# Fused cross-covariance attention and feed-forward kernel: start-up work reordered, w_in loaded in smaller blocks, four more stores halved

## The chip, the core and the metric

The kernel runs on one core of a Trainium2 chip. The metric is device time in microseconds (us) of that core, so lower is better. The core has a matrix engine (PE; its weight loads are listed as PEld), a vector engine (DVE), a scalar engine (ACT), a general engine that here mostly issues loads (POOL), and a queue engine (SP) that issues transposing loads and stores. Each engine runs its own instructions in program order, and engines wait for one another through semaphores. Transfers (DMA) run beside all of them.

## The reference, cut to what matters

```python
B, N, C = 4, 6080, 256           # q, k, v; D_ff = 2048
qn = q / (norm(q, axis=1) + 1e-6);  kn = k / (norm(k, axis=1) + 1e-6)
a  = softmax(kn.T @ qn / tau, axis=-1)      # 256 x 256 for each b
x  = (v @ a).reshape(24320, 256)
h  = x @ w_in                               # 24320 x 2048
g  = s * maximum(h, 0)**2 + b
out = g @ w_out                             # 24320 x 256
```

The kernel never forms x. It multiplies the small matrix a by w_in once for each of the four batches ("folding"), and then computes h directly as v times the folded weight `wa`.

## The kernel before, in words

**Two phases.** First the Gram matrix of batch 0 is built: q and k come in as chunks of rows (eleven of 512 rows and, at the end, two short ones of 256 and 192 rows), PE multiplies them (`mm`, L148), and ACT and DVE square them and add the squares up for the norms. Then 48 groups of at most 512 tokens are processed, 16 steps to a group, one step for each 128 columns of D_ff. The Gram matrices of batches 1 to 3 are built by side work within these steps.

**The end of the first phase, by hand.** Chunk squares are summed in a running tile `f` (the last addition is `into_first`, L205, on DVE). The last three chunks are "late": their squares are not summed but go to PE directly. `add_norms` (L238 for k, L242 for q) multiplies the sums and the late squares with a tile of ones on PE. `inverse` (L263) is four ACT instructions, first for k, then for q. `scale` (L288, DVE) multiplies the Gram matrix with the inverse norm of k, `exps` (L294, ACT) takes the exponential of its two halves j = 0, 1, scaled by the inverse norm of q, and `sums` (L304 on PE, L309 on DVE) gives the row sums and their reciprocal `rs`. `keep_busy` (L461) is a matmul whose result is not used.

**Folding.** For a block of columns f0 to f0+n and each half m of the rows of `wa`, `fold_mm` (L321) makes two matmuls, and `scaled` evacuates them with the factor `rs`: for m = 0 on ACT (L314), for m = 1 on DVE (L316). The first two blocks, 0 to 256 and 256 to 512, are folded before the first step of group 0; the blocks from 512, 1024 and 1536 on, 512 wide, are side work of the steps given in `FOLDS` (L555): 0, 0, 3, 4, 7, 8.

**A step.** In step m of group g, `mm1` (L641) makes two matmuls, which read columns 128 m to 128 m + 127 of both halves of `wa`, so step m waits for `scaled` of both engines on these columns. After each odd step ACT takes the maximum with zero of two steps' results (`relu`, L651, 128x1024), and in group 0 DVE squares that (`square`, L664). Side work comes last in a step, so a fold put into step 1 has its ACT and DVE evacuations behind the `relu` and the `square` of that step. From step 11 on group 0 also multiplies with w_out (`plain_mm2`, L713), and in step 12 the second group's v is transposed (`transpose_v`, L383). Groups 1 to 46 use seven products in place of eight (`seven_items`, L808).

**Buffers.** Accumulators of the folds, of `transpose_v` and of `plain_mm2` share three PSUM buffers (`ps_o`), the results of `mm1` two (`ps_h`).

**Loads and stores.** POOL issues all converting loads on one queue, in order: chunks of q and k, v of group 0, then w_in (`load_w_in`, L430) as columns 0 to 256, 256 to 512, 512 to 1024 and 1024 to 2048, then v of group 1 and w_out (L444). A finished group is stored (`store`, L676) by SP, the last group by ACT. The DMAs of SP and ACT take turns on eight semaphores, numbered 0 to 7 here. At the kernel's end SP waits for semaphores 0, 1, ... 7 one after the other. Group 46 (`NG - 2`) is stored in two halves.

Of the kernel before, what the change touches and what calls it, by code (L numbers as in the profile page):

```python
# [10 lines left out]
FP32 = mybir.dt.float32  # L11
# [6 lines left out]
def kernel(  # L18
# [12 lines left out]
    nc = tc.nc  # L31
    P = 128

    B, N, C = q.shape
# [56 lines left out]
    def h_tile(name):  # L91
        return ps_h.tile([P, 2, TG], FP32, tag="h_ps", name=name)
# [18 lines left out]
    class Gram:  # L111
# [134 lines left out]
        def finish_ops(self):  # L246
# [3 lines left out]
            def inverse(a=None):  # L250

                n = C + CH if a is None else (CH, C)[a]

                def part(i):
                    if i == 0:
                        st["r", a] = sm_pool.tile([P, n], FP32, tag=f"r{a}", name=f"r{a}")
                        if a is None:
                            st["r", 1], st["r", 0] = st["r", a][:, :C], st["r", a][:, C:]
                    r = st["r", a]
                    func, kw = [(AF.Ln, dict(bias=tiny)), (AF.Exp, dict(scale=0.5)),  # L260
                                (AF.Ln, dict(bias=eps)), (AF.Exp, dict(scale=-1.0))][i]
                    sums = self.n_all if a is None else self.n_ps[a]
                    po(nc.scalar.activation(out=r, in_=r if i else sums, func=func, **kw))  # L263
                    if i == 3 and a != 1 and inv_tau != 1.0:
                        po(nc.vector.tensor_scalar_mul(
                            out=st["r", 0], in0=st["r", 0], scalar1=inv_tau))

                return [lambda i=i: part(i) for i in range(4)]

            def norms(a):  # L270
                return lambda: self.add_norms(a, last=True)
# [39 lines left out]
            def scaled(f0, n, m, wa_ps):  # L311
                dst = self.wa[:, m, ds(f0, n)]
                if m == 0:
                    po(nc.scalar.mul(out=dst, in_=wa_ps, mul=st["rs"][:, m : m + 1]))  # L314
                else:
                    po(nc.vector.tensor_scalar_mul(  # L316
                        out=dst, in0=wa_ps, scalar1=st["rs"][:, m : m + 1]))

            def fold_mm(f0, n, m, wa_ps):
                for j in range(CH):  # L320
                    po(nc.tensor.matmul(wa_ps, st["e"][:, j, ts(m, P)],  # L321
                                        w_in16[:, j, ds(f0, n)],
                                        start=(j == 0), stop=(j == CH - 1)))

            def fold_both(f0, n):
                def f():

                    two = [self.bank("wa_ps", CH, C)[:, 0, :n], h_tile("wa_ps")[:, 0, :n]]
                    for m in range(CH):
                        fold_mm(f0, n, m, two[m])  # L330
                    for m in range(CH):
                        scaled(f0, n, m, two[m])
                return f

            def fold_one(f0, n, m):
                def f():
                    wa_ps = self.bank("wa_ps", CH, C).rearrange("p a c -> p (a c)")[:, :n]
                    fold_mm(f0, n, m, wa_ps)
                    scaled(f0, n, m, wa_ps)
                return f  # L340

            if self.b == 0:

                folds = [fold_both(0, 2 * P)]
                folds += [fold_one(2 * P, NW - 2 * P, m) for m in range(CH)]
            else:
                folds = []
            folds += [fold_one(f0, NW, m) for f0 in range(NW if self.b == 0 else 0, Dff, NW)
                      for m in range(CH)]
            if self.b == 0:  # L350
                front = [norms(1), *inverse(1), norms(0), *inverse(0), lambda: scale(CH)]
            else:
                front = [copy_out, norms_both, *inverse(), scale]
            return front + [lambda: exps(0), lambda: exps(1), sums] + folds

        def bank(self, name, a, b):

# [74 lines left out]
    load_v(0)  # L432
    load_w_in(0, 2 * P)
    load_w_in(2 * P, NW)
    load_w_in(NW, 2 * NW)
    load_w_in(2 * NW, Dff)
    w_out_rows = moe_w_out.rearrange("(fo p) d -> p fo d", p=P)
    load_v(1)
# [19 lines left out]
    def keep_busy(n):  # L458
# [3 lines left out]
                                stop=True, skip_group_check=True))  # L462

    norms_k, *rest = g0.finish_ops()
    inverse_k, norms_q, inverse_q, (scale_s, exps0, exps1, row_sums), folds = (
        rest[:4], rest[4], rest[5:9], rest[9:13], rest[13:])
    late = range(NCH0 - NLATE, NCH0)
    for c in range(NCH0 - NLATE):
        ops = g0.norm_ops(c)
        for j in range(g0.chunks[c][2]):  # L470
            g0.mm(c, j)
        keep_busy(FILL.get(c - NCH0, 0))
        for f in ops:
            f()

    ops = {c: g0.norm_ops(c) for c in late}
    for c in late:
        k_squares, _, into_rows = ops[c]
        k_squares()
        into_rows(1)  # L480
        if c < NCH0 - 1:
            g0.add_norms(1)
        else:
            norms_k()
    for f in inverse_k:
        f()
    for c in late:
        ops[c][1]()
        ops[c][2](0)
        for j in range(g0.chunks[c][2]):  # L490
            g0.mm(c, j)
        if c == NCH0 - 1:
            norms_q()
        else:
            g0.add_norms(0)
    for f in inverse_q:
        f()
    scale_s()
    transpose_v(0)
    keep_busy(1)  # L500
    for f in (exps0, exps1, row_sums, *folds[:3]):
        f()


# [47 lines left out]

    FIN = (0, 3, 5, 7, 9, 11, 13, 17, 19, 22)
    first_group = [b * N // TG for b in range(B)]
    FOLDS = (0, 0, 3, 4, 7, 8)  # L555
    for i, f in enumerate(folds[3:]):
        at_step(FOLDS[i], f)
    at_step(14, lambda: po(nc.vector.tensor_scalar_mul(
        out=s_out, in0=s_bc, scalar1=1.0 / (LAM * LAM))))
# [162 lines left out]
                    store(g)  # L722


    S = {}

    def sums_of(g, n, i0=0, i1=NP):
# [15 lines left out]
    def seven_items(g):  # L743
        st = {}
        lo, hi = slice(0, P), slice(P, C)
        G = lambda h, t: lambda: g_tiles[g][:, h, :, ts(t, TG // 2)]
        W = w_out16.rearrange("p (i h) c -> p h i c", h=2)
        U = lambda: upool.tile([P, 2, P], FP32, tag="u", name="u")

        def out_sb(t, half):  # L750
            if g not in o_sbs:
                o_sbs[g] = opool.tile([P, TG // P, C], FP32, tag="o_sb", name="o_sb")
            return o_sbs[g][:, ts(t, 2), half]

        def p1():
            st["u1"] = U()
            evacuate(st["u1"], st["X"], rowconst[:, lo], 1)

        def p5():
            st["u5"] = U()  # L760
            evacuate(st["u5"], st["Z"], rowconst[:, hi], 1)

        def p6():
            st["u2"] = U()
            evacuate(st["u2"], st["X"], rowconst[:, hi], 1)

        def p2():
            evacuate(out_sb(0, lo), st["Y"], st["u1"], 2)

        def p7():  # L770
            evacuate(out_sb(1, hi), st["X"], st["u5"], 2)

        def p3():
            evacuate(out_sb(0, hi), st["Z"], st["u2"], 2)
            if g == NG - 2:
                store(g, 0, 2)

        def p4():
            evacuate(out_sb(1, lo), st["X"], rowconst[:, lo], 1)
            store(g, 2 if g == NG - 2 else 0)  # L780

        def begin(name):
            t = ps_o.tile([P, 2, 2 * P], FP32, tag="o_ps", name="o_ps")
            halves = [t[:, h, :].rearrange("p (j c) -> p j c", j=2) for h in range(2)]
            if name == "X":
                st["X"] = halves[0]
            else:
                st["Z"], st["Y"] = halves

        products = [  # L790
            ("X", G(0, 0), W[:, 0, :, lo], p1),
            ("Z", lambda: S[1], T1, p5),
            ("X", lambda: S[2], T2, p6),
            ("Y", G(1, 0), W[:, 1, :, lo], p2),
            ("X", lambda: S[3], T3, p7),
            ("Z", lambda: S[4], W[:, 1, :, hi], p3),
            ("X", G(1, 1), N4, p4),
        ]
        items = []
        for n, (name, a, w, after) in enumerate(products):  # L800
            for i in range(NP):
                for j in range(2):
                    def f(n=n, name=name, a=a, w=w, after=after, i=i, j=j):
                        first = n < 2 and i == 0 and j == 0
                        if first:
                            begin(name)
                        last = i == NP - 1 and j == 1
                        po(nc.tensor.matmul(st[name][:, j, :], a()[:, i, ts(j, P)], w[:, i, :],  # L808
                                            start=first, stop=last, skip_group_check=True))
                        if last:  # L810
                            after()
                    items.append(f)
        return items
# [86 lines left out]
```

## Time and profile before

| | us |
|---|---|
| median of four runs (lowest, highest) | 719.36 (719.31, 719.47) |
| the profiled execution's own time | 719.29 |
| its span in the profile | 717.5 |
| first `mm1` starts | 37.77 |
| PE busy, whole span | 697.1 |
| last DVE instruction starts | 713.72 |
| last store is issued | 714.2 |

Times in the profile count from the span's start; the execution's own time is 1.79 us longer than the span, for what lies around it. A timeline row gives start, duration, engine, line, operation, output<-inputs and shapes; in brackets stands the idle time just before it and what ended it. Rows that hold several instructions ("x2") run from the first one's start to the last one's end. Matmuls overlap: 512 columns take 0.38 us each but follow each other every 0.22 us.

### The profile page before, as it was taken

What the parts mean: (1) busy time and instruction counts of PE and PEld (TensorE: products, weight loads), DVE (VectorE), ACT (ScalarE), POOL (GpSimd) and SP (SyncE); (2) the same over time, 40 slices, a digit from 0 to 9 for tenths busy, and PEclk for the clock granted to TensorE, in tenths of its full rate; (3) what the DMA queues carried; (4) which work ended last, traced back from release to release, by engine and by line L of the source; (5) the groups of instructions that cost most, each with busy time, mean ns of one, the idle gap of its engine ahead of it and who ended that gap; (6) DMA issues with size and microseconds to landing.
All of it is one profiled execution on the core that took longest, in us unless ns stands there. A gap on an engine that the chain in (4) does not pass through costs nothing.

```text
span 717.5 us, 17472 instructions
## 1 busy us (share of the span) xinstructions
PE 697.1 (97%) x7419; PEld 503.7 (70%) x7419; DVE 622.2 (87%) x871; ACT 545.8 (76%) x593; POOL 110.5 (15%) x188
## 2 busy tenths in 40 slices
PE   4699999999999999999999999999999999999997
PEld 2456777776677777777677777777668777777777
DVE  4879999988789989998889899998887888888886
ACT  5789877787777777778777778777877777877874
POOL 4532332102102222111010222110000000000000
PEclk9999999999999999999999999999999999999999
DMA  9999999636555978444682888943323323321201
GB/s 236 206 260 178 149 178 133 119 92 124 119 116 109 136 134 144 112 89 94 138 145 53 148 132 126 153 90 82 93 64 74 97 67 75 100 57 51 76 32 74
DMA packets 86606, 83.47 MB, mean 116 GB/s; under 512 B 56224, under 2 KB 61664, under 8 KB 86528
## 3 DMA queue, kind: packets, MB, share of 16 engines
q0 software_dynamic: 26336, 43.40, 37.7%
q1 hardware_dynamic: 59616, 37.64, 21.8%
q8 instruction: 58, 0.95, 0.5%
q10 hardware_dynamic: 576, 1.31, 0.5%
q14 instruction: 20, 0.16, 0.1%
HBM read 78.91 MB, written 24.90 MB: 145 GB/s over the span
## 4 chain that ended last, share of the span: by engine, by line
PE 92%; DMA 4%; DVE 2%; ACT 1%; issue 0%; POOL 0%; DVEq 0%; ACTq 0%
PE h_ps L641 45%; PE o_ps L808 40%; PE s_ps L148 4%; PE wa_ps L321 2%; DMA qk<-in_k_dram 1%; DMA w_in<-in_moe_w_in_dram 1%; DMA raw<-in_q_dram 1%; PE o_ps L713 1%; ACT sq L177 1%; DVE f L191 1%; PE o_ps L687 0%; ACT r L651 0%; DVE sq L174 0%; DVE o_sb L669 0%; POOL w_in L430 0%
## 5 line engine op out<-in xcount | busy, mean ns | idle before, releaser
L651 ACT ACTIVATE r<-h_ps 128x1024 f16<-128x1024 f32 (+1 forms) x384 | 388.5, 1014 | 150.8 <-PE h_ps L641 146.1
L641 PE MATMUL h_ps<-vT,wa 128*128 128x512 f16 (+7 forms) x1632 | 452.0, 364 | 0.1
L808 PEld LDWEIGHTS <-S 128*128 128x128 f16 x2944 | 198.0, 98 | 84.7 <-issue 0.4
L808 PEld LDWEIGHTS <-g 128*128 128x128 f16 x2208 | 155.1, 98 | 74.1
L664 DVE TENSOR_TENSOR g<-r 128x2048 f16<-128x2048 f16 (+2 forms) x150 | 174.6, 1164 | 15.5 <-ACT r L651 15.0
L808 PE MATMUL o_ps<-T,S 128*128 128x128 f16 x2208 | 183.3, 219 | 0.1
L641 PEld LDWEIGHTS <-wa 128*128 128x128 f16 x1632 | 136.0, 98 | 20.5 <-DVE wa L316 0.2
L808 PE MATMUL o_ps<-w_out,g 128*128 128x128 f16 x1472 | 134.2, 219 | 0.2 <-DVE u L669 0.2
L669 DVE SCALAR_TENSOR_TENSOR o_sb<-o_ps,s_out,u 128x256 f32<-128x256 f32 x138 | 66.3, 481 | 50.8 <-PE o_ps L808 48.8
L662 ACT ACTIVATE g<-r 128x1024 f16<-128x1024 f16 (+1 forms) x97 | 100.3, 1034 | 0.2
L148 PE MATMUL s_ps<-qk 128*128 128x256 f16 (+1 forms) x384 | 71.7, 289 | 13.7 <-ACT qk L139 9.0
L372 POOL DMA_DIRECT2D v<-in_v_dram x48 | 31.3, 655 | 265.4 <-DMA vT<-v 208.6
L669 DVE SCALAR_TENSOR_TENSOR u<-o_ps,s_out,rowconst 128x256 f32<-128x256 f32 x138 | 65.8, 477 | 0.0
L808 PE MATMUL o_ps<-w_out,S 128*128 128x128 f16 x736 | 63.5, 219 | 0.0
L808 PE MATMUL o_ps<-N,g 128*128 128x128 f16 x736 | 63.4, 219 | 0.0
L207 POOL DMA_DIRECT2D f<-f x30 | 26.3, 878 | 224.5 <-DVE f L191 188.4
L737 DVE TENSOR_TENSOR S<-S,g 128x2048 f16<-128x2048 f16 (+1 forms) x47 | 56.4, 1201 | 1.3
L177 ACT ACTIVATE sq<-qk 128x1024 f16<-128x1024 f16 (+2 forms) x53 | 54.5, 1041 | 3.9 <-DMA qk<-in_k_dram 2.3
L735 DVE TENSOR_TENSOR S<-g 128x2048 f16<-128x2048 f16 (+1 forms) x47 | 56.0, 1192 | 0.0
L741 DVE TENSOR_TENSOR S<-g,S 128x2048 f16<-128x2048 f16 x46 | 55.9, 1214 | 0.0
L739 DVE TENSOR_TENSOR S<-g 128x2048 f16<-128x2048 f16 x46 | 55.8, 1214 | 0.0
L148 PEld LDWEIGHTS <-qk 128*128 128x128 f16 (+1 forms) x384 | 33.0, 103 | 20.4 <-ACT qk L139 9.4
(76 smaller groups left out, 312.9 us busy)
## 6 DMA issues: line engine op xcount, KB each, us to landing
out_dram<-o_sb SPq DMA_DIRECT2D x46, 512.0 KB, 3.0
v<-in_v_dram POOLq DMA_DIRECT2D x47, 256.0 KB, 4.8
qk<-in_k_dram POOLq DMA_DIRECT2D x42, 256.0 KB, 6.2
qk<-in_q_dram POOLq DMA_DIRECT2D x42, 256.0 KB, 7.1
f<-f POOLq DMA_DIRECT2D x30, 128.0 KB, 3.1
vT<-v SPq DMA_TRANSPOSE x182, 3.0
w<-in_moe_w_out_dram POOLq DMA_DIRECT2D x4, 512.0 KB, 11.2
raw<-in_k_dram SPq DMA_DIRECT2D x2, 512.0 KB, 6.6
```

Source lines behind the costliest of these rows:

```text
L148: po(nc.tensor.matmul(self.s_ps[:, ch, :], qc[:np_, j, ts(ch, P)], kc[:np_, j, :], start=(c == 0 and j == 0 and ch == 0), stop=(c == len(s ...
L177: po(nc.scalar.activation(out=st["sq"][:np_, a, js, :], in_=(qc, kc)[a][:np_, js, :], func=AF.Square))
L641: po(nc.tensor.matmul(dst, wa[:, ci, ts(m, P)], src, start=(ci == 0), stop=(ci == CH - 1), skip_group_check=True))
L651: po(nc.scalar.activation(out=r16[:, :, i % 2, :n], in_=h_tiles.pop((g, i))[:, :, :n], func=AF.Relu))
L662: po(nc.scalar.activation(out=dst, in_=src, func=AF.Square))
L664: po(nc.vector.tensor_mul(dst, src, src))
L669: po(nc.vector.scalar_tensor_tensor(out=dst, in0=src, scalar=s_out, op0=ALU.mult, in1=add, op1=ALU.add))
L735: po(nc.vector.tensor_add(T[1], A21, A22))
L737: po(nc.vector.tensor_sub(T[2], T[1], A11))
L739: po(nc.vector.tensor_sub(T[3], A11, A21))
L741: po(nc.vector.tensor_sub(T[4], A12, T[2]))
L808: po(nc.tensor.matmul(st[name][:, j, :], a()[:, i, ts(j, P)], w[:, i, :], start=first, stop=last, skip_group_check=True))
```

## The change

Four things change:

- The running sum `f` is multiplied last instead of first in k's norms, and its last addition on DVE comes after the square of the last k chunk. The norm matmuls of q's last chunk come before that chunk's Gram matmuls.
- The first fold block (0 to 256) is made half by half: after exponential j, PE makes the row-sum matmuls and the fold matmuls of that half. `scaled` of this block works on 128 columns at a time.
- The columns 512 to 1024 of w_in are loaded and folded as two blocks of 256. The eight folds left for group 0's steps stand in steps 1, 1, 3, 3, 5, 6, 8, 9.
- Groups 1 to 4 are stored in two halves too. That is four more DMAs on SP, so the last store moves from semaphore 3 to semaphore 7.

```diff
-            def fold_both(f0, n):
...
+            def first_block(n):
+                two = [self.bank("wa_ps", CH, C)[:, 0, :n], h_tile("wa_ps")[:, 0, :n]]
+                r_ps = self.bank("r_ps", CH, C)[:, :, 0]
+                for j in range(CH):
+                    exps(j)
+                    for ch in range(CH):
+                        po(nc.tensor.matmul(r_ps[:, ch : ch + 1], st["e"][:, j, ts(ch, P)],
...
                     for m in range(CH):
-                        fold_mm(f0, n, m, two[m])
+                        po(nc.tensor.matmul(two[m], st["e"][:, j, ts(m, P)],
+                                            w_in16[:, j, :n],
+                                            start=(j == 0), stop=(j == CH - 1)))
+                st["rs"] = sm_pool.tile([P, CH], FP32, tag="rs", name="rs")
+                po(nc.vector.reciprocal(out=st["rs"], in_=r_ps))
+                for f0 in range(0, n, P):
                     for m in range(CH):
-                        scaled(f0, n, m, two[m])
-                return f
+                        scaled(f0, P, m, two[m][:, ds(f0, P)])
...
-                folds = [fold_both(0, 2 * P)]
-                folds += [fold_one(2 * P, NW - 2 * P, m) for m in range(CH)]
+                blocks = [(2 * P, 2 * P), (4 * P, 2 * P), (6 * P, 2 * P), (2 * NW, NW), (3 * NW, NW)]
...
-    load_w_in(NW, 2 * NW)
+    load_w_in(NW, 6 * P)
+    load_w_in(6 * P, 2 * NW)
     load_w_in(2 * NW, Dff)
...
+        if c == NCH0 - NLATE - 1:
+            ops, last_sum = ops[:-1], ops[-1]
         for f in ops:
             f()
+    sum_rows = [rows.pop() for rows in g0.rows]
     ops = {c: g0.norm_ops(c) for c in late}
     for c in late:
         k_squares, _, into_rows = ops[c]
         k_squares()
         into_rows(1)
-        if c < NCH0 - 1:
-            g0.add_norms(1)
-        else:
-            norms_k()
-    for f in inverse_k:
+        g0.add_norms(1)
+    last_sum()
+    for rows, row in zip(g0.rows, sum_rows):
+        rows.append(row)
+    for f in (norms_k, *inverse_k):
         f()
     for c in late:
         ops[c][1]()
         ops[c][2](0)
+        if c == NCH0 - 1:
+            norms_q()
         for j in range(g0.chunks[c][2]):
             g0.mm(c, j)
-        if c == NCH0 - 1:
-            norms_q()
-        else:
+        if c < NCH0 - 1:
             g0.add_norms(0)
...
-    for f in (exps0, exps1, row_sums, *folds[:3]):
+    for f in (first_block, *folds[:2]):
         f()
...
-    FOLDS = (0, 0, 3, 4, 7, 8)
-    for i, f in enumerate(folds[3:]):
+    FOLDS = (1, 1, 3, 3, 5, 6, 8, 9)
+    for i, f in enumerate(folds[2:]):
         at_step(FOLDS[i], f)
...
+    HALVES = (1, 2, 3, 4, NG - 2)
...
         def p3():
             evacuate(out_sb(0, hi), st["Z"], st["u2"], 2)
-            if g == NG - 2:
+            if g in HALVES:
                 store(g, 0, 2)
         def p4():
             evacuate(out_sb(1, lo), st["X"], rowconst[:, lo], 1)
-            store(g, 2 if g == NG - 2 else 0)
+            store(g, 2 if g in HALVES else 0)
```

More of the change, by code (lines that the diff above doesn't have):

```diff
@@ L323, in fold_mm @@
                                         start=(j == 0), stop=(j == CH - 1)))
-            def fold_both(f0, n):
-                def f():
-                    two = [self.bank("wa_ps", CH, C)[:, 0, :n], h_tile("wa_ps")[:, 0, :n]]
-                    for m in range(CH):
-                        fold_mm(f0, n, m, two[m])
+            def first_block(n):
[5 more added lines that the diff above has]
+                        po(nc.tensor.matmul(r_ps[:, ch : ch + 1], st["e"][:, j, ts(ch, P)],
+                                            parts16, start=(ch == 0 and j == 0),
+                                            stop=(ch == CH - 1 and j == CH - 1),
+                                            skip_group_check=True))
+                    for m in range(CH):
+                        po(nc.tensor.matmul(two[m], st["e"][:, j, ts(m, P)],
[4 more added lines that the diff above has]
+                for f0 in range(0, n, P):
                     for m in range(CH):
-                        scaled(f0, n, m, two[m])
-                return f
+                        scaled(f0, P, m, two[m][:, ds(f0, P)])
             def fold_one(f0, n, m):
@@ L342, in finish_ops @@
             if self.b == 0:
-                folds = [fold_both(0, 2 * P)]
-                folds += [fold_one(2 * P, NW - 2 * P, m) for m in range(CH)]
-            else:
-                folds = []
-            folds += [fold_one(f0, NW, m) for f0 in range(NW if self.b == 0 else 0, Dff, NW)
-                      for m in range(CH)]
+                blocks = [(2 * P, 2 * P), (4 * P, 2 * P), (6 * P, 2 * P), (2 * NW, NW), (3 * NW, NW)]
+            else:
+                blocks = [(f0, NW) for f0 in range(0, Dff, NW)]
+            folds = [fold_one(f0, n, m) for f0, n in blocks for m in range(CH)]
             if self.b == 0:
-                front = [norms(1), *inverse(1), norms(0), *inverse(0), lambda: scale(CH)]
-            else:
-                front = [copy_out, norms_both, *inverse(), scale]
-            return front + [lambda: exps(0), lambda: exps(1), sums] + folds
+                return [norms(1), *inverse(1), norms(0), *inverse(0), lambda: scale(CH),
+                        lambda: first_block(2 * P)] + folds
+            return [copy_out, norms_both, *inverse(), scale, lambda: exps(0), lambda: exps(1),
+                    sums] + folds
         def bank(self, name, a, b):
@@ L464 @@
     norms_k, *rest = g0.finish_ops()
-    inverse_k, norms_q, inverse_q, (scale_s, exps0, exps1, row_sums), folds = (
-        rest[:4], rest[4], rest[5:9], rest[9:13], rest[13:])
+    inverse_k, norms_q, inverse_q, scale_s, first_block, folds = (
+        rest[:4], rest[4], rest[5:9], rest[9], rest[10], rest[11:])
     late = range(NCH0 - NLATE, NCH0)
@@ L489 @@
         ops[c][2](0)
+        if c == NCH0 - 1:
+            norms_q()
         for j in range(g0.chunks[c][2]):
             g0.mm(c, j)
-        if c == NCH0 - 1:
-            norms_q()
-        else:
+        if c < NCH0 - 1:
             g0.add_norms(0)
-    for f in inverse_q:
+    for f in (*inverse_q, scale_s):
         f()
-    scale_s()
     transpose_v(0)
     keep_busy(1)
-    for f in (exps0, exps1, row_sums, *folds[:3]):
+    for f in (first_block, *folds[:2]):
         f()
```

## The prediction

> **What bounds the kernel now.** I read the chain of waits first, then PE's waits by stretch, then the engines' timelines from 30 to 50 us, and at last the records after the last matmul. All times are in us of the profiled execution.
>
> The chain of work that ended last, in order of time, starts with loads:
>
> ```profile
> 30.03 1.40 POOL w_in L430 x2
> 31.43 9.37 DMA w_in<-in_moe_w_in_dram
> 40.80 0.04 issue
> 40.84 0.59 PE wa_ps L321 x2
> 41.44 0.43 PE h_ps L641 x2
> ```
>
> Up to 40.80 the end is set by the last block of w_in; from there on by PE. PE's waits between 73 and 712 are one, of 0.2:
>
> ```profile
> PE o_ps L808 <- DVE u L669: 0.2, 1, 0.2
> ```
>
> So what PE loses or gains before 73 arrives whole at the end. Between 46 and 73 ACT (51.57 to 56.36) and DVE (63.75 to 72.76) are on the chain, but each is started by a matmul of PE, so a late PE moves them too. The change is therefore worth what it does to the first `mm1`, to PE's waits inside group 0, and to the tail.
>
> Which load the first `mm1` waits for stands in the timeline of weight loads (columns as in the section before):
>
> ```profile
> 37.28 0.33 PEld L321 LDWEIGHTS <-eT 128*128 128x128 f16 x4 [0.17 <-DMA w_in<-in_moe_w_in_dram]
> 37.76 0.30 PEld L641 LDWEIGHTS <-wa 128*128 128x128 f16 x2
> ```
>
> The fold of columns 256 to 512 waits for its load (issued at 30.03, 7.2 to landing: 37.24), and the first `mm1` stands behind it.
>
> **Part 1, norms and first block: about 0.04 gained, the rest is covered.** Before, PE waits 1.22 for the sum `f` and starts k's nine norm matmuls at 31.29; ACT's inverse starts at 32.47. After, the squares go first as they come (ACT's end at 30.83 and 31.34, DVE's of the last chunk at 30.93 + 0.41 = 31.34), and `f` ends one 0.35 slot later, at 31.71, so its matmul runs 31.83 to 32.10 and ACT starts at 32.13: 0.34 earlier. Its four instructions then end at 34.05, not 34.39. The norms of q end at 34.06 instead of 34.61, and ACT's four short instructions (1.06 in all, 34.65 to 35.71 before) end at 35.16. The Gram matmuls still end at 34.53, `scale` gives its first half at 35.05, so the exponentials start at 35.19, not 35.74: 0.55 earlier. PE makes the first half at 35.75 to 36.19 and the second at 36.16 to 36.60, the reciprocal ends at 36.57, and the first 128 columns of `wa` are ready near 37.1 (a 128-wide evacuation isn't in the trace: between 0.17 for two columns and 0.48 for 256, I take 0.37). But the fold of 256 to 512 still comes before the first `mm1`, and still waits for 37.24. It takes 4 x 0.11 from 37.29 on, so `mm1` starts at 37.73, not 37.77. The cover is that load; if it came when the other parts were ready, `mm1` would start at 37.08, and 0.65 more would be gained.
>
> **Part 2, the smaller block of w_in: nothing.** One more issue costs POOL 0.72, hidden in the 6 to 9 that each load waits in the queue. The price of the smaller pieces I bound from the landings: blocks of 256 columns follow one another by 0.66 to 0.74, and the 512 columns took 1.24, so the last block lands 0.1 to 0.24 later, near 41.0. Its fold now comes at 41.65 (below). The 0.4 that PE waited before 40.84 goes, and I count it in part 3. By the Trainium skill ("DMA: Bandwidth & Descriptors", section Anatomy of one DMA) a DMA pays about 2.0 us once whatever its size; taken as a price for one more DMA this would put the last block at 42.8 and cost 1.2. The spacing of 0.7 is what this queue shows, which is never empty here, and I go by it.
>
> **Part 3, the folds in later steps: about 1.55 lost.** Both engines work in order, so where a fold stands in a step decides. Before, the evacuation of columns 512 to 1024 came ahead of the first `relu` and `square`:
>
> ```profile
> 38.92 0.69 ACT L314 ACTIVATE wa<-wa_ps,rs 128x512 f16<-128x512 f32 x1 [0.73 <-PE wa_ps L321]
> 39.78 1.94 ACT L651 ACTIVATE r<-h_ps 128x1024 f16<-128x1024 f32 x2 [0.18 <-PE h_ps L641]
> ```
> ```profile
> 39.35 0.75 DVE L316 TENSOR_SCALAR wa<-wa_ps,rs 128x512 f16<-128x512 f32 x1 [0.93 <-PE wa_ps L321]
> 40.84 0.69 DVE L664 TENSOR_TENSOR g<-r 128x1024 f16<-128x1024 f16 x1 [0.74 <-ACT r L651]
> 41.75 0.69 DVE L664 TENSOR_TENSOR g<-r 128x1024 f16<-128x1024 f16 x1 [0.22 <-ACT r L651]
> 42.36 0.75 DVE L316 TENSOR_SCALAR wa<-wa_ps,rs 128x512 f16<-128x512 f32 x1
> ```
>
> After, each DVE evacuation is queued behind a `square`, that behind a `relu`, and that behind two `mm1`. From the end of an odd step to usable columns this takes relu 1.02 + square 0.61 (to the next start) + evacuation 0.48 (256) or 0.75 (512) + 0.13 for three signals: 2.24 or 2.51. PE has less to do in between. I walk PE through it with the rows' durations (a step 0.43, a fold of 256 half as much: 0.22, ends 0.38 or 0.27 after the last start):
>
> - Steps 0, 1 from 37.73, ending at 38.76; `relu` 38.80 to 39.82, `square` 39.86, evacuation of 512 to 768 on DVE 40.47 to 40.95. PE meanwhile makes two folds, steps 2, 3, two folds (0.13 of waiting for a buffer) and is at the second matmul of step 4 at 40.68: it waits until 41.00, 0.32.
> - Step 6 needs columns 768 to 896, ready on DVE at 42.35 behind the second `square`: 0.10.
> - Step 8 needs columns from 1024. The third `relu` follows step 5 (41.81), 41.85 to 42.87; `square` 42.91, evacuation 43.52 to 44.27. PE is there at 43.72 and waits until 44.32: 0.60.
> - Step 12 needs columns from 1536. Step 9 ends at 45.56; ACT first has its own half of that block, 45.17 to 45.86, then `relu` to 46.88, `square` 46.92, evacuation 47.53 to 48.28. PE is there at 47.34 and waits until 48.33: 0.99.
>
> Together 2.14. Before, the same stretch had 0.59 of waiting (0.09 and 0.39 for w_in, the rest for w_out and step 12). Step 12 before already touches this wait:
>
> ```profile
> 46.74 0.10 PEld L641 LDWEIGHTS <-wa 128*128 128x128 f16 x1 [0.23 <-DVE wa L316]
> ```
>
> 2.14 - 0.59 = 1.55 lost. Step 13 starts at about 49.4, not 47.86. Nothing later takes it back: ACT's `relu` at 48.49 (1.20 idle before it) and DVE's `square` at 49.55 both wait for step 13, and what follows hangs on them.
>
> **Part 4, the halved stores and the tail: 0.60 gained.** Four more issues of 0.33 on SP lie in its long waits for DVE (376.8 in all), ahead of the transposing loads as before. The last store is issued at 714.23 and lands at 715.99. SP's own semaphore instructions after that:
>
> ```profile
> L895 SPq EVENT_SEMAPHORE  x6: 17/28/28, 716.0 to 716.9; - x6
> L895 SPq DRAIN  x2: 7/7/7, 716.7 to 716.7; - x2
> ```
>
> After the landing SP passes semaphore 3 at 716.01 and then 4, 5, 6, 7 until 716.61, all long complete, and ends at 716.67. With the last store on semaphore 7 these are passed earlier, and one wait is left: 0.06 instead of 0.66. Bounds: 0.23 (without the one step of 0.37 among them, should it stay) to 0.60. I take 0.60, as SP reaches the waits earlier in any case.
>
> **Sum.** 719.29 - 0.04 + 1.55 - 0.60 = 720.2. This is against the profiled execution; the median of the runs is 0.07 higher, so I name 720.3, that is 0.13% more than before. Less than 0.2% (1.44) can't be told from no change.
>
> **Rivals.**
>
> - *The load isn't late.* The profile's DMA table shows one instruction fetch of 16 KB between 35 and 36; the load of 256 to 512 had landed on 15 of its 16 engines by 35.89, on the last at 37.24. Should this fetch fall elsewhere, part 1 gives 0.65 more: 719.6. Against it: PE's instructions keep their numbers, and the delayed engine carries the delay on. Chance 0.13.
> - *The evacuations aren't late.* If the order matters less than I think (ACT and DVE quicker, columns ready by PE's arrival), PE keeps only about 0.1 of waiting: 719.29 - 0.04 - 0.49 - 0.60 = 718.2; with the first rival 717.5. For it: the first `relu` starts a full 0.98 earlier. Against: four waits would all have to be off, two of them by 0.6 or more. Chance 0.17, of which 0.05 is below 717.92.
> - *Slower: PE loses its clock.* In the table by stretches of 3.41 the clock is 0.50 in one, after one in which PE was busy for 1.34 of 3.41; with 2.20 busy it stayed at 1.00. The waits of part 3 put holes into the stretch from 47.05 to 50.46. If they leave PE under about 2.0 busy there, the next 3.41 run at half speed: 1.7 more, 722.0. My walk leaves 2.4 or more. Chance 0.07.
> - *The tail doesn't move* (SP's waits are not in that order, or the step of 0.37 moves behind the last): 720.6 to 720.9. Chance 0.10.
>
> The forecast has 0.53; its own spread is about 0.5, from the 0.1 or so in each of the four waits. The range reaches down to the second rival's edge and up past the fourth: 718.5 to 721.3. Faster by over 0.2% has 0.05; slower (above 720.80: the third rival, half of the fourth, the forecast's upper part) 0.20; within, 0.75.
>
> **What would show it.** Right: first exponential near 35.2 and first `mm1` near 37.7; a weight load of L641's counterpart waiting for DVE's evacuation of `wa` three times between 40 and 49, the longest near 1.0 ahead of step 12; no wait for w_in after 38; the last landing followed by the end within 0.9 instead of 1.5. Wrong: `mm1` near 37.1, or PE without waits for `wa`, or a clock of 0.50 in any stretch after 26.57.

## The result, and the profile after

| | before | after |
|---|---|---|
| median of the runs, us (lowest to highest) | 719.38 (719.19 to 719.94, 60 runs) | 720.35 (720.11 to 720.59, 42 runs) |
| profiled execution, its span | 719.29, 717.5 | 720.49, 718.7 |
| first `mm1` starts | 37.77 | 38.07 |
| step 13 of group 0 starts | 47.86 | 49.69 |
| last store's landing to the span's end | 1.53 | 0.91 |

After takes 1.0013 times as long as before, interval 1.0009 to 1.0017: 0.97 us more. Forecast was 720.3.

In the profiles the span grows by 1.2, and three differences add up to it: the first `mm1` comes 0.30 later, from there to step 13 it takes 11.61 in place of 10.09 (1.52 more), and the tail is 0.62 shorter. Between step 13 and the last `mm1` matmul both take the same 662.25.

The chain of work that ended last, of after. The columns are start, us and what; `mm1` is L652 here, `relu` L662, `square` L675, the reordered block L332 (row sums) and L337 (fold), the evacuations still L314 and L316.

```profile
29.12 7.76 DMA w_in<-in_moe_w_in_dram
36.88 0.04 issue
36.92 0.39 PE wa_ps L337 x2
...
38.07 1.05 PE h_ps L652 x4
39.12 0.02 issue
39.15 1.03 ACT r L662
40.18 0.03 issue
40.20 0.69 DVE g L675
40.90 0.41 DVE wa L316
41.30 0.05 issue
41.35 0.83 PE h_ps L652 x3
```

Where before had one load and then PE, after has a ring: `mm1`, `relu`, `square`, evacuation, and only then the next `mm1`. The chain runs through it three times, to 41.35, 44.67 and 48.58. No load of w_in is on the chain after 36.88. The same in the timeline of weight loads of after (what ended the wait stands in brackets):

```profile
36.92 0.11 PEld L337 LDWEIGHTS <-eT 128*128 128x128 f16 x2 [0.75 <-DMA w_in<-in_moe_w_in_dram]
...
38.07 0.55 PEld L652 LDWEIGHTS <-wa 128*128 128x128 f16 x4 [0.33 <-ACT wa L314]
...
41.34 0.33 PEld L652 LDWEIGHTS <-wa 128*128 128x128 f16 x3 [0.55 <-DVE wa L316]
...
42.65 0.10 PEld L652 LDWEIGHTS <-wa 128*128 128x128 f16 x1 [0.32 <-DVE wa L316]
...
44.67 0.10 PEld L652 LDWEIGHTS <-wa 128*128 128x128 f16 x1 [0.71 <-DVE wa L316]
...
48.58 0.10 PEld L652 LDWEIGHTS <-wa 128*128 128x128 f16 x1 [1.09 <-DVE wa L316]
```

Four weight loads wait for DVE's evacuation, at steps 4, 6, 8 and 12; before had one such wait, of 0.23. A weight load waits ahead of its matmul, so not all of this is lost. PE's matmuls themselves wait three times (from 34 to 73: 1.3 in all, 0.7 the longest):

```profile
PE h_ps L652 <- DVE wa L316: 1.3, 3, 0.7
```

The ends of matmuls are modelled; counted from start to start (0.22 where nothing waits), steps 4, 8 and 12 lose 0.33, 0.72 and 0.87, and step 6 nothing. The first line of the timeline was not forecast: the first block itself now waits for w_in.

SP's own instructions at the end of after (first and last start at the right of the durations):

```profile
L907 SPq EVENT_SEMAPHORE  x11: 17/28/28, 714.2 to 718.6; - x11
...
L907 SPq DRAIN  x3: 7/7/7, 717.9 to 718.2; - x3
```

The last store lands at 717.80, and SP drains at 717.9. Before, the landing at 715.99 was followed by 0.6 us of other semaphores until the drain at 716.7.

### The profile page after: what moved, and what is told of

Same layout as the page of the kernel before. It is cut to its first block, busy times and chain, and to the rows that moved or that the text cites. A ratio compares the mean times of both kernels' runs of the same rounds, so it can differ in the third digit from the quotient of the medians.

```text
span 718.7 us, 17493 instructions
## 1 busy us (share of the span) xinstructions
PE 699.3 (97%) x7423; PEld 504.4 (70%) x7423; DVE 622.3 (87%) x873; ACT 546.2 (76%) x595; POOL 111.1 (15%) x189
## 4 chain that ended last, share of the span: by engine, by line
PE 91%; DMA 4%; DVE 2%; ACT 1%; POOL 1%; issue 0%; POOLq 0%; ACTq 0%
PE h_ps L652 44%; PE o_ps L820 40%; PE s_ps L148 4%; DMA qk<-in_k_dram 2%; PE wa_ps L321 2%; DMA qk<-in_q_dram 1%; DMA w_in<-in_moe_w_in_dram 1%; ACT r L662 1%; PE o_ps L724 1%; POOL qk L132 1%; PE o_ps L698 0%; DVE g L675 0%; DVE wa L316 0%; DVE o_sb L680 0%; DVE S L749 0%
## 5 line engine op out<-in xcount | busy, mean ns | idle before, releaser
L662 ACT ACTIVATE r<-h_ps 128x1024 f16<-128x1024 f32 (+1 forms) x384 | 388.8, 1014 | 152.0 <-PE h_ps L652 147.1
L652 PE MATMUL h_ps<-vT,wa 128*128 128x512 f16 (+7 forms) x1632 | 452.8, 364 | 1.4 <-DVE wa L316 1.3
L675 DVE TENSOR_TENSOR g<-r 128x2048 f16<-128x2048 f16 (+2 forms) x150 | 174.6, 1164 | 17.2 <-ACT r L662 16.8
L652 PEld LDWEIGHTS <-wa 128*128 128x128 f16 x1632 | 135.8, 98 | 22.6 <-DVE wa L316 2.7
```

The lines of the kernel that those rows point to most:

```text
L652: po(nc.tensor.matmul(dst, wa[:, ci, ts(m, P)], src, start=(ci == 0), stop=(ci == CH - 1), skip_group_check=True))
L662: po(nc.scalar.activation(out=r16[:, :, i % 2, :n], in_=h_tiles.pop((g, i))[:, :, :n], func=AF.Relu))
L675: po(nc.vector.tensor_mul(dst, src, src))
```

## The experiments

My theory was that of the forecast: the late folds cost 1.5, the tail gives 0.6, the rest is nothing. Differences named below are to before in the same comparison, where no other kernel is named. An interval such as 0.9991 to 1.0009 is 0.65 us to each side, so a smaller difference in the times is not clear of noise by itself and stands on the rows of the profile beside it.

**Part 4 alone** (`tail_alone`): before, with the halved stores.

```diff
+    HALVES = (1, 2, 3, 4, NG - 2)
...
-            if g == NG - 2:
+            if g in HALVES:
...
-            store(g, 2 if g == NG - 2 else 0)
+            store(g, 2 if g in HALVES else 0)
```

> The kernel before with only the halved stores of groups 1 to 4, so that the last store takes the last semaphore. Theory (the folds' place costs 1.55, the tail gives 0.60): 719.4 - 0.6 = 718.8, and the end comes 0.9 after the last landing instead of 1.5. Rival (the tail doesn't move, and the whole change costs about 1.0 in one place): 719.4.

718.72 (ratio 0.9991, 0.9983 to 1.0000): 0.66 less. From the landing to the end it takes 0.91 instead of 1.53, which is the same 0.62 as in after.

**Part 3 alone** (`late_folds_alone`): before, with the folds in the later steps and its loads as they were.

```diff
-            folds += [fold_one(f0, NW, m) for f0 in range(NW if self.b == 0 else 0, Dff, NW)
-                      for m in range(CH)]
+            blocks = ([(4 * P, 2 * P), (6 * P, 2 * P), (2 * NW, NW), (3 * NW, NW)]
+                      if self.b == 0 else [(f0, NW) for f0 in range(0, Dff, NW)])
+            folds += [fold_one(f0, n, m) for f0, n in blocks for m in range(CH)]
...
-    FOLDS = (0, 0, 3, 4, 7, 8)
+    FOLDS = (1, 1, 3, 3, 5, 6, 8, 9)
```

> The kernel before with only the folds of columns 512 to 2048 in blocks of 256, 256, 512, 512 at steps 1, 1, 3, 3, 5, 6, 8, 9; loads, norms, first block and stores as before. Theory: PE waits four times for the evacuations of wa, 2.1 in all against 0.6, so 719.4 + 1.5 = 720.9. Rival (the loss comes from the first block or the loads ahead of the first step): 719.4 or a little less, since the wait for the last block of w_in goes.

721.21 (1.0028, 1.0018 to 1.0038): 1.83 more. The first `mm1` to step 13 takes 11.61, the same as in after, and the waits are after's:

```profile
PEld L642 <- DVE wa L316: 2.7, 4, 1.1
```

(PE's weight loads of `mm1` waiting for DVE's evacuation, from 35 to 51: 2.7 in all, four times, 1.1 the longest.) So the order makes them, whatever the loads and the first block are. Of the profiled execution's difference 1.52 lies between the first `mm1` and step 13, the rest ahead of it: the first `mm1` comes 0.36 later, and q's last chunk had landed 0.37 later (33.64, before 33.27). That landing moves from one execution to the next: `tail_alone`, `tail_44` and before, which have the same instructions up to it, have it at 33.56, 33.20 and 33.27.

**After without part 3** (`early_folds`): after, with the eight folds as early as before's.

```diff
-    FOLDS = (1, 1, 3, 3, 5, 6, 8, 9)
+    FOLDS = (0, 0, 0, 0, 3, 4, 7, 8)
```

> The changed kernel with the folds back ahead of the first relu: steps 0, 0, 0, 0, 3, 4, 7, 8. Theory: the three waits of 0.3 to 1.0 for the evacuations go, the wait of 0.3 to 0.5 for the last block of w_in at step 3 comes back, the tail's 0.6 stays: 718.8 to 719.0. Rival (the loss lies ahead of the first step): it stays near 720.3.

718.79 (0.9992, 0.9984 to 1.0001), 1.56 less than after. First `mm1` to step 13: 9.96.

**Parts 1 and the first block alone** (`front_alone`): after, with the stores, the loads and the folds' steps of before.

```diff
-                blocks = [(2 * P, 2 * P), (4 * P, 2 * P), (6 * P, 2 * P), (2 * NW, NW), (3 * NW, NW)]
+                blocks = [(2 * P, 2 * P), (NW, NW), (2 * NW, NW), (3 * NW, NW)]
...
-    load_w_in(NW, 6 * P)
-    load_w_in(6 * P, 2 * NW)
+    load_w_in(NW, 2 * NW)
...
-    FOLDS = (1, 1, 3, 3, 5, 6, 8, 9)
+    FOLDS = (0, 0, 3, 4, 7, 8)
...
-    HALVES = (1, 2, 3, 4, NG - 2)
+    HALVES = (NG - 2,)
```

> The kernel before with only the reordered norms and the first block made half by half; loads of w_in, folds and stores as before. Theory: the exponentials start about 0.5 earlier and nothing comes of it, because the loads of columns 256 to 512 and 512 to 1024 land as before: 719.35 to 719.5. Rival (the first block now waits for the load of columns 0 to 256, and that sets the loss): first step 0.3 later, 719.7 or more. If the loads were no cover: 718.7.

719.37 (1.0000, 0.9991 to 1.0009): nothing, as forecast. But the cover is another load: here as in after the fold of columns 0 to 256 waits for w_in (0.8), not the fold of 256 to 512.

**One evacuation one step earlier** (`one_step_earlier`): after, with the last fold in step 8.

```diff
-    FOLDS = (1, 1, 3, 3, 5, 6, 8, 9)
+    FOLDS = (1, 1, 3, 3, 5, 6, 8, 8)
```

> The changed kernel with one entry changed: the second fold of columns 1536 to 2048 at step 8 instead of 9, so that its evacuation on DVE is queued behind the square of step 7 instead of that of step 9. Theory: the wait of about 1.0 ahead of step 12 goes and nothing else changes: 720.35 - 1.0 = 719.35. Rival (the loss is spread over the later folds' matmuls or lies ahead of the first step): 720.2 to 720.4.

719.43 (1.0000, 0.9991 to 1.0010), 0.92 less than after. Only one number in a list differs. The weight loads' waits for DVE's evacuation go from 2.7 (four) to 1.6 (three), and step 12's is the one that is gone.

**All folds in even steps** (`even_steps`): after, with two folds in each of steps 0, 2, 4, 6, where side work is behind no `relu`.

```diff
-    FOLDS = (1, 1, 3, 3, 5, 6, 8, 9)
+    FOLDS = (0, 0, 2, 2, 4, 4, 6, 6)
```

> The changed kernel with all folds at even steps, 0, 0, 2, 2, 4, 4, 6, 6, where no relu or square stands ahead of them in the step. Theory: no wait for wa between steps 1 and 12; against the folds at 0, 0, 0, 0, 3, 4, 7, 8 (718.8) the wait for a buffer in step 0 (0.3) and for the last block of w_in (0.4) go as well: 718.2, faster than both kernels. Rival (what is left is set by the loads and the later engines): 718.8.

719.13 (0.9997, 0.9988 to 1.0006): my 718.2 missed by 0.9. First `mm1` to step 13 is 10.42. The timeline of ACT in this kernel:

```profile
40.80 1.02 ACT L662 ACTIVATE r<-h_ps 128x1024 f16<-128x1024 f32 x1
41.72 0.68 ACT L314 ACTIVATE wa<-wa_ps,rs 128x512 f16<-128x512 f32 x1
42.53 1.02 ACT L662 ACTIVATE r<-h_ps 128x1024 f16<-128x1024 f32 x1
...
44.26 1.94 ACT L662 ACTIVATE r<-h_ps 128x1024 f16<-128x1024 f32 x2
```

and of PE:

```profile
45.33 1.02 PE L652 MATMUL h_ps<-vT,wa 128*128 128x512 f16 x4 [0.25 <-ACT r L662]
46.66 0.60 PE L724 MATMUL o_ps<-w_out,g 128*128 128x256 f16 x4 [0.31 <-DVE w_out L549]
```

ACT has no idle time from 40.42 to 46.20 (no row has brackets), and PE waits for its `relu` (0.25) instead of for DVE's evacuation; then 0.31 for a conversion of w_out that DVE comes to late. That is 0.56 of the 0.8 by which 10.42 is over the 9.62 seen below. I had taken one engine's wait away and not looked at how full the other would be.

**The small block alone** (`split_alone`): before, with 512 to 1024 loaded as two blocks and folded as one.

```diff
-    load_w_in(NW, 2 * NW)
+    load_w_in(NW, 6 * P)
+    load_w_in(6 * P, 2 * NW)
```

> The kernel before with only the load of columns 512 to 1024 cut in two. Theory: the last block lands 0.1 to 0.24 later, and here PE waits for it at step 3, so 719.4 + 0.1 to 0.24 = 719.5 to 719.6. Rival (a DMA more costs its fixed time): 720.5 or more. Rival (no cost): 719.4.

719.32 (1.0000, 0.9991 to 1.0009). My 719.5 to 719.6 missed; the rival without a cost fits. The last block lands at 40.83, before at 40.80. Fifteen of its sixteen DMA engines are through at 40.03, before at 39.67, and in this execution q's last chunk had landed 0.31 later (33.58), which leaves 0.05. One more DMA in a queue that is never empty costs nothing more that can be seen here. The Trainium skill's 2.0 us for each DMA ("DMA: Bandwidth & Descriptors", Anatomy of one DMA), taken as a price for one more DMA, would by estimate have put it near 42.8.

**Fewer norm matmuls** (`fewer_norm_matmuls`): `even_steps`, with most of the late chunks' squares left out of the norms, 30 matmuls and weight loads fewer on PE (the result is another one). It asks if the instruction fetch that delays w_in hangs on PE's instruction numbers.

```diff
-                    self.rows[a].append((st["sq"], np_, jc))
+                    self.rows[a].append((st["sq"], np_, 1))
```

> The kernel with the folds at even steps, in which of each late chunk's squares only the first of two or four rows' part goes into the norms (the others are left out of the sums), 30 PE instructions fewer ahead of the first fold. Theory (PE's 16 KB instruction fetch, bound to an instruction's number, falls on one of the 16 DMA engines and delays each load of w_in queued there by about 1.1): the fetch comes 1.5 or more later, after 36, the block 0 to 256 then lands within 0.1 of its other 15 engines, near 35.4, the first step starts 0.5 to 0.8 earlier, near 37.2, and the time is 0.3 to 0.8 below that of even_steps. Rival (the late engine is slow for another reason): the last engine of the block 0 to 256 or 256 to 512 is still 1.1 late, and the first step starts near 37.9.

719.14 (1.0000, 0.9991 to 1.0009), as much as `even_steps`. The fetch still comes at 34.68, and the first 256 columns of w_in still land on their last DMA engine 1.36 after the other fifteen (36.81 and 35.45). So it doesn't hang on the number alone, and the kernel wins nothing: its expectation missed. Its profiled execution took 720.68, its nine others 719.01 to 719.62. The table by stretches of that execution shows what was different (start:end, us, then busy time and instructions of PE, PEld, DVE, ACT and POOL, the granted clock, DMA share, GB/s):

```profile
33.80:37.20 3.40, 2.28 (x26) 1.47 (x24) 1.49 (x4) 2.23 (x7) 1.56 (x3) 1.00 1.39 199
37.20:40.60 3.40, 3.40 (x17) 1.94 (x15) 1.60 (x5) 1.49 (x4) 2.59 (x4) 0.51 1.13 226
```

One stretch at half clock, after one in which PE was busy for 2.28, goes with about 1.5 more (720.68 against the median of 719.14). That is the forecast's third rival, in another place.

**The cover taken away, twice.** Without the load of v of group 0 all later loads come some 1.27 earlier. Group 0 takes k rows of the first late chunk in its place (so its output is another one). `front_no_v0` is `front_alone` without this load, `before_no_v0` is before without it.

```diff
+    v_tiles[0] = g0.raw[len(g0.chunks) - NLATE][:, 0]
-    load_v(0)
```

> The reordered norms and the reordered first folded block alone, with the load of v of group 0 left out: group 0 takes k rows of the first late chunk in place of its v, so the output of group 0 is another one, and all later loads come earlier by about 1.27 us, the time of that load. My theory: what covers the worth of the new order is the landing of w_in. With the load gone w_in's first 256 columns land near 34.0 and the next near 34.7, before the norms are through, and the first h matmul starts near 37.1, by the norms and the block alone. Rival: the first step is set by something else that follows the norms (the evacuations of the first block, the code fetch of TensorE), and it stays near 37.9 and no earlier than in the kernel before with the same load left out.

> The kernel before with the same load left out (the output of group 0 is another one). My theory: here the first h matmul is set by its own chain, near 37.76 as before, so that the new order is worth about 0.65 us once the loads are out of the way: this kernel about 719.3, the one with the new order about 718.7. Rival: no difference between the two, because the first step waits for the same thing in both.

718.39 (0.9987, 0.9979 to 0.9996) and 718.97 (0.9995, 0.9986 to 1.0004): the reordering is worth 0.58 once no load hides it (the runs do not overlap: 718.23 to 718.68 and 718.80 to 719.59). PE's timeline, first of `front_no_v0`:

```profile
36.28 0.20 PE L332 MATMUL r_ps<-parts,eT 128*128 128x1 f16 x2 [0.50 <-ACT eT L294]
...
36.74 0.38 PE L337 MATMUL wa_ps<-w_in,eT 128*128 128x256 f16 x2
36.96 0.60 PE L321 MATMUL wa_ps<-w_in,eT 128*128 128x256 f16 x4
37.61 0.61 PE L651 MATMUL h_ps<-vT,wa 128*128 128x512 f16 x2
```

then of `before_no_v0`:

```profile
36.99 0.23 PE L304 MATMUL r_ps<-parts,eT 128*128 128x1 f16 x3 [0.22 <-ACT eT L294]
37.08 1.03 PE L321 MATMUL wa_ps<-w_in,eT 128*128 128x256 f16 x8
38.05 0.60 PE L641 MATMUL h_ps<-vT,wa 128*128 128x512 f16 x2
```

No row waits for w_in in either. I had expected 37.1 and 37.76; the loads of these two executions ran 0.52 and 0.31 later than in before's (q's last chunk landed at 33.79 and 33.58, not 33.27), which leaves 37.09 and 37.74. From that landing on, the first `mm1` comes 3.82 and 4.47 later: 0.65 apart, the forecast's number. Of this the norms bring 0.52 (1.93 and 2.45 to the first exponential) and the first block made half by half 0.13 (1.89 and 2.02 from there to the first `mm1`). Both take 9.62 from there to step 13, as w_in's last block is early too. That is 0.47 less than before, and why even `before_no_v0` gains 0.43.

**Two better lists of steps.** `tail_44` is `tail_alone` with the third block folded in step 4, so that the wait for w_in's last block falls away. `after_01` is after with a list between `early_folds` and the loads.

```diff
-    FOLDS = (0, 0, 3, 4, 7, 8)
+    FOLDS = (0, 0, 4, 4, 7, 8)
```

> The kernel before with the halved stores and the third folded block moved to the step of the fourth (0, 0, 4, 4, 7, 8): takes the wait of TensorE for the last block of w_in, 0.3 to 0.4 us at step 3, out of the way. My theory: 718.4, that is 0.3 less than with the halved stores alone (718.7). Rival: 718.7, since two blocks evacuated together at step 4 come as late as the load did; or above 719 when the evacuations hold ScalarE, as with two blocks in each even step.

718.82 (0.9992, 0.9983 to 1.0001): no better than `tail_alone`. The waits of PE between 38 and 45 were `wa_ps` for w_in (0.2) in before; in `tail_44` they are:

```profile
PEld L641 <- issue: 0.5, 1, 0.5
...
PE h_ps L641 <- ACT r L651: 0.2, 1, 0.2
```

The load's wait is gone, and step 4 stands at 40.75 for a free `mm1` buffer, which the first `relu` gives back just then (39.68 and 1.02 more). In before that wait lay hidden under the load's (40.80).

```diff
-    FOLDS = (1, 1, 3, 3, 5, 6, 8, 9)
+    FOLDS = (0, 0, 0, 1, 4, 4, 7, 8)
```

> The changed kernel with its eight blocks folded at the steps 0, 0, 0, 1, 4, 4, 7, 8: takes the wait for a free buffer at step 0 (0.30 us, where four blocks are folded in step 0) out of the way. My theory: 718.5, 0.3 less than with 0, 0, 0, 0, 3, 4, 7, 8 (718.8). Rival: 718.8 or more, since the block moved to step 1 is waited for there.

718.58 (0.9989, 0.9980 to 0.9998): 0.82 less than before and 1.77 less than after, the lowest median here of a kernel that computes all of the reference, though not clear of `tail_alone` (718.72) by the runs. First `mm1` to step 13: 9.82, 0.14 less than in `early_folds`; step 4 waits for the first `relu` here too, until 41.04.

## Why the prediction was right

**What bounds the kernel: right.** "What PE loses or gains before 73 arrives whole at the end" held to 0.02: from step 13 to the last `mm1` matmul all fourteen profiled kernels take 662.25 to 662.27, whether step 13 starts at 47.23 or at 49.90. Differences in group 0 can therefore be read off at step 13.

**Part 1: right in sum, but by another load, and that is luck.** The reordered norms gave what was worked out: from the landing of q's last chunk (33.56, before 33.27) to the first exponential it takes 1.94 in after and 2.47 in before, 0.53 less (forecast 0.55). The exponentials of after, then of before:

```profile
35.50 0.91 ACT L294 ACTIVATE eT<-sm_t,r 128x256 f16<-128x256 f32 x2
...
35.74 0.91 ACT L294 ACTIVATE eT<-sm_t,r 128x256 f16<-128x256 f32 x2
```

From the exponential to the first `mm1` the forecast's 1.89 is what `front_no_v0` shows. What failed is a sub-step: "PE makes the first half at 35.75 to 36.19 and the second at 36.16 to 36.60", with the load of 256 to 512 as the cover. The 16 KB instruction fetch, which I had placed between 35 and 36 as before, came at 34.70 in after (before at 35.10), and so met the block 0 to 256 in place of the next one: fifteen engines had landed it by 35.52, the last at 36.88. The first half waited until 36.92, and the first `mm1` started at 38.07 instead of 37.73. Of these 0.34, 0.29 is that the loads as a whole ran later in this execution. Measured from q's last chunk the first `mm1` is where it was (4.51 later, before 4.50). The first rival asked for a fetch that falls elsewhere, and it did; its argument against, that PE's instructions keep their numbers, was beside the point, as `fewer_norm_matmuls` showed. But it fell on a load that covers as much, which the forecast had not weighed; had it come after both blocks, part 1 would by that rival's own sum have given 0.65 more.

**Part 2: right.** No cost, shown alone; the 0.1 to 0.24 by which the last block was to land later is not seen either (0.05, `split_alone`).

**Part 3: right, in mechanism and size.** 1.55 forecast, 1.52 in the profile, 1.56 by taking it out and 1.83 by doing it alone (its interval, 1.3 to 2.7, holds both; 0.36 of it lies ahead of the first `mm1`). The walk, beside after's rows:

| | forecast | after |
|---|---|---|
| step 0 | 37.73 | 38.07 |
| first `relu`, first `square` | 38.80, 39.86 | 39.15, 40.20 |
| step 4 released by DVE | 41.00 | 41.34 |
| step 8 released | 44.32 | 44.67 |
| step 12 released | 48.33 | 48.58 |
| step 13 | 49.4 | 49.69 |

All are 0.25 to 0.35 later, as step 0 is (0.34). The second rival would have needed the releases to be earlier than PE's arrival; with step 0's 0.34 taken off, each was within 0.1 of the walk. The single waits of PE are less exact than their sum: the walk had 0.32, 0.10, 0.60 and 0.99 for steps 4, 6, 8 and 12, and after lost 0.33, nothing, 0.72 (0.13 of it for ACT's half, which the walk left out) and 0.87. The two DVE rows that set the last release, of after:

```profile
47.17 0.69 DVE L675 TENSOR_TENSOR g<-r 128x1024 f16<-128x1024 f16 x1 [0.88 <-ACT r L662]
47.78 0.75 DVE L316 TENSOR_SCALAR wa<-wa_ps,rs 128x512 f16<-128x512 f32 x1
```

DVE is idle for 0.88 ahead of the `square`, though the fold's matmuls are through at 46.35 (45.76 and 0.59), because its order says `square` first and `square` wants `relu`. `one_step_earlier` moves only this fold and takes 0.92 back.

**Part 4: right.** 0.60 forecast, 0.62 in the profile, 0.66 alone. The fourth rival is out.

**Clock.** In after the clock stays at 1.00 through group 0, as forecast. But one sign named for a wrong forecast did come, a clock of 0.50 after 26.57: in after it is at half from 23.3 to 30.1, in before only from 23.16 to 26.57. The second half of that stretch (columns as in the table by stretches above):

```profile
26.70:30.10 3.40, 3.40 (x15) 2.19 (x14) 2.70 (x6) 2.14 (x3) 1.63 (x3) 0.50 1.15 206
```

This stretch ends before q's last chunk lands, and that landing doesn't follow the clock: kernels that kept 1.00 there have it at 33.20 (`tail_44`) and 33.79 (`front_no_v0`), after at 33.56. So it costs nothing that shows, and the sign was drawn too wide: it should have named group 0. My bound ("under about 2.0 busy") is not safe either: `fewer_norm_matmuls` lost the clock after 2.28.

**Sum.** 719.29 + 0.01 + 1.52 - 0.62 = 720.20, and with the 0.09 by which before's median is above its profiled execution, 720.29. The runs' 720.35 is 0.06 above; I have no row for that rest.

## What to carry to other kernels

On engines that work in order, the step a piece of side work stands in decides what it waits for: behind a `relu` that waits for this step's own matmuls, an evacuation of 0.48 to 0.75 was usable only 2.2 to 2.5 us after the step's last matmul, and moving one list entry by one gave 0.92 back. Walk the bounding engine through each step with the release times of the others, and do it for every other engine too: `even_steps` and `tail_44` took one wait away and met the next at once. A reordering that brings nothing may be sound work under a late transfer; take the transfer away in an experiment before it is given up.

## What was not expected of the hardware

- One fetch of 16 KB of instructions (0.98 on one DMA engine) goes with a late landing of a load that is spread over sixteen. In all fourteen profiled kernels the block of w_in that is landing when it comes, or the next one, is the first to land 0.92 to 1.46 later on one engine than on the others (in the blocks ahead of it 0.31 at most), and the blocks behind it still land 0.59 to 1.25 later on one engine (1.14 for the one that before waits for at 40.80). That the fetch is PE's is worked out: the profile of after has 58 of them and 14846 matmuls and weight loads of PE, one for every 256. It comes 0.6 to 0.8 ahead of the first exponential in all fourteen, at 34.49 to 35.46. What sets it off stays open; it isn't PE's instruction number alone.
- Busy time alone doesn't tell when the clock falls. `fewer_norm_matmuls` fell to 0.51 after a stretch with PE busy for 2.28 of 3.40, and before kept 1.00 after one with 2.20, `even_steps` after one with 1.58 (17.97 to 21.39). The Trainium skill ("TensorE: Matmul & The Clock Gate", What's actually happening) names an idle window of about 3.4 us as the cause; the length of one stretch agrees with these rows, but the window ahead of it was not idle. What the gate counts was not settled here.
